# New orders at both ends of a fused attention and soft-MoE kernel, and queries loaded by one transfer per pair

## The chip, the cores and the metric

The kernel runs on one core of a Trainium2 chip. The metric is the device time in microseconds of one execution. A core has five engines with a queue of instructions each: TensorE (PE), VectorE (DVE), ScalarE (ACT), GpSimd (POOL) and SyncE (SP); SP does nothing here but issue transfers, which 16 DMA engines carry out. Engines wait for each other through semaphores.

## What is computed

Attention over 8 batches, 8 heads, 576 positions, 64 columns, where scores more than tau below their row's maximum are dropped, and then a soft mixture of experts over all 4608 positions (512 columns, 8 experts with 4 slots each, hidden size 1024):

```python
scores = scale * q @ k.T
thresh = scores.max(-1) - tau
scores = where(scores >= thresh, scores, -1e9)
attn = softmax(scores)
x = (attn @ v)                       # to (4608, 512)
logits = x @ phi                     # phi (512, 32)
d = softmax(logits, axis=0)          # over the 4608 positions
slot_input = d.T @ x                 # (32, 512)
for e in range(8):                   # 4 slots each
    slot_out[e] = relu(slot_input[e] @ w1[e]) @ w2[e]
c = softmax(logits, axis=1)
out = c @ slot_out                   # (4608, 512)
```

## The kernel before

The 64 heads are worked off as 32 pairs of heads, the two heads of a pair in the two halves of the 128 partitions, or with one half for each half of the keys. Pair p of batch b = p // 4 has nine groups of queries. Per group: PE multiplies q by k (L776; the ninth group L781) into one of four PSUM regions; DVE copies the scores out with the sign turned and takes the row's extreme (L788); ACT takes the exponential (L798); POOL makes the threshold (L801); DVE masks and sums (L804). Then PE transposes the weights (recorded at L692), ACT copies them to pTa, pTb and pTl (L697), and PE multiplies them by v (L894), 256 and 320 queries at a time. The result is transposed back, scaled and kept as x and xT. After the fourth pair of a batch the dispatch follows: logits (L976), running maximum (L982, L985), exponentials dT and f (L989, L987), weighing of x into acc (L1024, L1029, L1037). When the last batch is done, the slot inputs (L948) are made and the tail starts, in an order written by hand: hidden layer (L1200), second layer (L1234), combination (L1276), stores.

Loads: q, k and vv have two buffers each. The load of a pair's q waits for the last q·k product of the pair two before it, k's likewise, and vv's for the last product with v. All loads after the first pair's stand in SP's queue, one after the other: what is behind a waiting load waits too. DMA semaphores go round eight, so a load also waits for the landing of the eighth before it. k is loaded in two halves (L740, 64 rows of 2 x 288) and then scaled by POOL (L756). q has the same 64 rows in both halves of the partitions, since the two halves of the array work on different keys with the same queries. 26 of 64 weight tiles of 512 KB are preloaded during the attention (w, L672); 20 more (host) go into attention buffers that have become free, and 18 follow into w buffers after their first use.

The order: every instruction up to the tail is put down with `G.add(engine, duration, nominal time, function, reads, writes)` in the class Order. `plan()` sorts each engine's instructions by a number, from TABLE where there is one, places them one by one and gives out the buffers. So TABLE's numbers are a fixed order for each engine's queue, SP's included, and nothing is moved at run time. The planner counts 4500 ns from an SP issue to its data for every load, whatever its shape (`LAT`). TABLE is keyed by scopes: "first" and "last" for the first and last pair, "pair0" to "pair3" for the middle ones (with a, y, z for the first and the last two batches), "batch", "end", "load..", "new..", and "soft" for the softmax over the slots. FILL (14 double) and WARM (17 single) are 128x128 transposes of the identity without use for the result, placed on PE at the start and near the end.

The queries of a pair, in before:

```python
for g in range(2 if p else 0):
    G.add("SP", 1250 if p < 3 else 800, t0 - 18 + hs[0], lambda g=g, a=hs[0], z=hs[-1] + 1: nc.sync.dma_start(
        qt.t[rows[g], a:z], qT[b, j, :, a:z]), w=[qt[h, g] for h in hs])
```

where `rows` is the two halves of the partitions, `qT[b, j]` is 64 x 2 x 576 and `qt` is a tile of 128 x 2 x 576.

Of the kernel before, what the change touches and what calls it, by code (L numbers as in the profile page):

```python
# [34 lines left out]
WARM = 17  # L35
# [3 lines left out]
for _n, _v in (  # L39
    ("first", [  # L40
# [7 lines left out]
    ]),  # L48
# [8 lines left out]
    ]),  # L57
# [8 lines left out]
    ]),  # L66
# [9 lines left out]
    ]),  # L76
# [476 lines left out]
def softmax_attention_soft_moe(  # L553
# [815 lines left out]
```

## Time and profile before

| | |
|---|---|
| time, median of 3 runs | 546.99 us (546.82 to 549.59) |
| profiled execution | 546.67 us |
| its span | 544.9 us (1.8 us lie around it) |
| PE, DVE, ACT, POOL busy | 524.9, 469.6, 456.9, 243.4 us |
| loaded and stored by DMA | 83.03 MB, 152 GB/s in the mean |
| first product q·k on PE | 5.68 us |
| hidden layer begins (L1200) | 482.28 us |

In a row of time the first number is the start in us from the begin of the span, the second the duration; then come engine, line, operation, what is written and what is read (`out<-in`), shape and count. In brackets stands how long the engine was idle before and what released it. SPq is the issue of a transfer on SP's queue; the transfer itself comes later. Matmuls are pipelined and their ends are modelled, so rows of PE overlap a little.

### The profile page before, as it was taken

To read this page: it belongs to the slowest core of one execution; us is meant where nothing else is said; L and a number is where in the kernel's file an instruction comes from. 1 tells how busy PE (TensorE), PEld (TensorE's weight loads), DVE (VectorE), ACT (ScalarE), POOL (GpSimd) and SP (SyncE) were. 2 spreads that over 40 slices of the span, in tenths; PEclk is the share of its full clock that TensorE was granted. 3 is DMA by queue.
4 is the path that set the end of the run, shared out by engine and by line. 5 is a ranking of instruction groups with operands and counts; after the bars stand their busy time and mean duration, and the time that the engine had idled before them with its cause. 6 is when DMAs were issued, how large, how long until landed. Compare 5 with 4: busy or idle time off the path is not lost.

```text
span 544.9 us, 18241 instructions
## 1 busy us (share of the span) xinstructions
PE 524.9 (96%) x6994; PEld 335.8 (62%) x6994; DVE 469.6 (86%) x1326; ACT 456.9 (84%) x786; POOL 243.4 (45%) x475
## 2 busy tenths in 40 slices
PE   8999999999999999999999999999999999999990
PEld 6666666666666666666666666666666656644470
DVE  6999998999999999999899989999999999522192
ACT  3999998999899989998999989999999888621180
POOL 3554555554545454545355545545454624121030
PEclk9999999999999999999999999999999999999996
DMA  7256555555535553333233333333333303999498
GB/s 182 69 165 172 168 167 169 165 164 165 174 91 168 166 161 119 96 85 91 71 91 92 90 92 92 91 91 91 91 91 92 89 5 141 348 410 410 188 371 321
DMA packets 31990, 83.03 MB, mean 152 GB/s; under 512 B 4640, under 2 KB 12832, under 8 KB 31904
## 3 DMA queue, kind: packets, MB, share of 16 engines
q1 hardware_dynamic: 31584, 81.43, 48.6%
q8 instruction: 55, 0.90, 0.7%
q10 hardware_dynamic: 320, 0.44, 0.3%
q14 instruction: 31, 0.25, 0.2%
HBM read 72.42 MB, written 9.44 MB: 150 GB/s over the span
## 4 chain that ended last, share of the span: by engine, by line
PE 86%; ACT 5%; DVE 5%; issue 2%; DMA 1%; SPq 0%; DVEq 0%; ACTq 0%
PE ps L894 29%; PE ps L776 24%; PE ps L692 17%; PE ps L781 3%; PE h L1200 3%; PE so L1234 2%; PE ps L918 2%; PE ps L976 2%; PE ps L1024 1%; DVE p L804 1%; ACT pTb L697 1%; DVE cT L1192 1%; DVE host L1280 1%; ACT pTa L697 1%; ACT p L798 1%
## 5 line engine op out<-in xcount | busy, mean ns | idle before, releaser
L788 DVE TENSOR_SCALAR_CACHE_REDUCE ss<-ps 128x576 f32<-128x576 f32 x288 | 208.3, 751 | 15.5 <-ACT pTl L697 4.8
L801 POOL TENSOR_SCALAR thr<-nmx,pabs 128x1 f32<-128x1 f32 x288 | 132.6, 462 | 185.0 <-DVE ss L788 164.8
L804 DVE SCALAR_TENSOR_TENSOR p<-ss,thr,p 128x576 f32<-128x576 f32 x256 | 201.3, 821 | 4.0 <-ACT p L798 3.8
L798 ACT ACTIVATE p<-ss,nmx 128x576 f32<-128x576 f32 x256 | 188.1, 780 | 15.1 <-DVE ss L788 15.0
L776 PE MATMUL ps<-k,q 64*128 64x288 f32 x1024 | 167.1, 427 | 1.4 <-DMA q<-in_qT 0.5
L692 PE MATMUL ps<-ident,p 64*128 64x64 f32 x2304 | 97.7, 223 | 1.3 <-ACT pTa L697 1.0
L692 PEld LDWEIGHTS ps<-ident,p 64*128 64x128 f32 x2304 | 88.0, 138 | 17.5 <-ACT pTa L697 3.1
L776 PEld LDWEIGHTS ps<-k,q 64*128 64x128 f32 x1024 | 83.3, 188 | 22.6 <-ACT pTl L876 5.8
L697 ACT COPY pTb<-ps 128x1024 f32<-128x1024 f32 (+1 forms) x96 | 84.0, 876 | 5.0 <-PE ps L692 3.1
L894 PE MATMUL ps<-pTb,vv 128*64 128x320 f32 x512 | 76.0, 439 | 0.4 <-DVE pTl L876 0.4
L697 ACT COPY pTa<-ps 128x1024 f32<-128x1024 f32 x64 | 64.9, 1017 | 0.4 <-PE ps L692 0.4
L894 PE MATMUL ps<-pTa,vv 128*64 128x256 f32 x512 | 62.3, 385 | 0.0
L894 PEld LDWEIGHTS ps<-pTb,vv 128*64 128x64 f32 x512 | 34.1, 136 | 36.4 <-issue 8.9
L894 PEld LDWEIGHTS ps<-pTa,vv 128*64 128x64 f32 x512 | 34.0, 136 | 26.2 <-DVE ss L788 8.5
L894 PE MATMUL ps<-pTl,vv 128*64 128x256 f32 (+1 forms) x256 | 41.9, 406 | 0.0
L913 POOL TENSOR_TENSOR x<-x,ri 128x512 f32<-128x512 f32 x31 | 32.3, 1042 | 4.7 <-ACT x L697 4.7
L697 ACT COPY xT<-ps 128x256 f32<-128x256 f32 (+1 forms) x62 | 24.7, 398 | 6.3 <-PE ps L894 5.3
L894 PEld LDWEIGHTS ps<-pTl,vv 128*64 128x64 f32 x256 | 18.5, 137 | 12.6
L804 DVE SCALAR_TENSOR_TENSOR pL<-ss,thr,pL 128x576 f32<-128x576 f32 x32 | 26.0, 813 | 0.0
L798 ACT ACTIVATE pL<-ss,nmx 128x576 f32<-128x576 f32 x32 | 24.8, 775 | 0.5 <-DVE ss L788 0.5
L1169 POOL TENSOR_TENSOR c<-lall,crow 128x512 f32<-128x512 f32 x9 | 9.3, 1046 | 35.5 <-PE ct L684 35.5
L756 POOL TENSOR_SCALAR k<-k,flag 128x576 f32<-128x576 f32 x31 | 25.1, 809 | 0.2
(137 smaller groups left out, 536.8 us busy)
## 6 DMA issues: line engine op xcount, KB each, us to landing
w<-in_w SPq DMA_DIRECT2D x44, 512.0 KB, 7.0
q<-in_qT SPq DMA_DIRECT2D x62, 288.0 KB, 4.6
vv<-in_vt SPq DMA_DIRECT2D x32, 320.0 KB, 4.9
host<-in_w SPq DMA_DIRECT2D x20, 512.0 KB, 7.4
k<-in_kT SPq DMA_DIRECT2D x62, 144.0 KB, 3.1
out<-w SPq DMA_DIRECT2D x8, 512.0 KB, 3.7
out<-host SPq DMA_DIRECT2D x8, 512.0 KB, 5.1
out<-host SPq DMA_DIRECT2D x4, 256.0 KB, 4.5
```

The lines of the kernel that those rows point to most:

```text
L692: nc.tensor.transpose(out=s[:, g, c:c + 64], in_=ins[g], identity=ident[rows[g], rows[g]], tile_position=(64 * g, 0))
L697: G.add("ACT", 51 + 0.833 * n, nom, lambda: nc.scalar.copy(*io()), r, w)
L756: sc = lambda e, kc=kc: lambda: e.tensor_scalar(out=kt.t[:, kc], in0=kt.t[:, kc], scalar1=flag8, **one)
L776: nc.tensor.matmul(s.t[:, g, 0:HS], qt.t[rows[g], h, c * 128:(c + 1) * 128], kt.t[rows[g], h * HS:(h + 1) * HS], start=True, stop=True, ti ...
L781: nc.tensor.matmul(s.t[rows[a], g, 0:HS], qt.t[rows[g], a, SM:S], kt.t[rows[g], a * HS:(a + 1) * HS], start=True, stop=True, tile_position ...
L788: dve(674, t + OFF['mx'], [s], [ss, nmx], lambda s=s, ss=ss, nmx=nmx: nc.vector.tensor_scalar(out=ss.t.rearrange("p (a k) -> p a k", a=2), ...
L798: G.add("ACT", 668, t + OFF['ex'], lambda sv=sv, nmx=nmx, view=view: nc.scalar.activation(view().rearrange("p (a k) -> p a k", a=2), sv(), ...
L801: pool(250, t + OFF['th'], lambda nmx=nmx, thr=thr: nc.gpsimd.tensor_scalar(out=thr.t, in0=nmx.t, scalar1=1.0, scalar2=pabs, op0=ALU.mult, ...
L804: fn=lambda sv=sv, thr=thr, view=view, i=i: nc.vector.scalar_tensor_tensor(out=view().rearrange("p (a k) -> p a k", a=2), in0=sv(), scalar ...
L894: nc.tensor.matmul(lone(w)[h * 64:(h + 1) * 64, 0:n], vv.t[:, v0:v0 + 64], p0, start=(kb == 0), stop=(kb == 4), tile_position=(0, h * 64), ...
L913: G.add("POOL", 1040, u + 6.8, own=f"new{j}" + group(b), r=[ri[0]], w=[x[j]], fn=lambda: nc.gpsimd.tensor_tensor(out=wide(), in0=wide(), i ...
L1200: nc.tensor.matmul(hp[n][g * 32:(g + 1) * 32, :], siT[:, kb, :], t[g][:, n * 512:(n + 1) * 512], start=(kb == 0), stop=(kb == 3), tile_pos ...
```

## The change

Three things change: TABLE's numbers for the first and the last pair, for the dispatch and the softmax, for the loads and for the middle pairs too; WARM; and the load of q.

```diff
-WARM = 17
+WARM = 13
...
     ("first", [
-        -29145.8, -29045.8, 5200, -28845.8, -28745.8, -28645.8, 7150, 3900, 6450, 7520, 8376, 8414, 16050.4, 9956,
+        -18044.4, -29045.8, 5200, -12489.2, -28745.8, -26707.8, 7150, -12484.5, 6450, 7520, -17331.8, 7943.7, 17078.1,
...
-            for g in range(2 if p else 0):
-                G.add("SP", 1250 if p < 3 else 800, t0 - 18 + hs[0], lambda g=g, a=hs[0], z=hs[-1] + 1: nc.sync.dma_start(
-                    qt.t[rows[g], a:z], qT[b, j, :, a:z]), w=[qt[h, g] for h in hs])
+            if p:
+                G.add("SP", 1250 if p < 3 else 800, t0 - 18, lambda: nc.sync.dma_start(
+                    qt.t.rearrange("p h s -> p (h s)"),
+                    qT[b, j].rearrange("d h s -> d (h s)").unsqueeze(0).to_broadcast([2, D, 2 * S])),
+                    w=[qt[h, g] for h in hs for g in range(2)])
+                G.skip(1)
```

Before, each of the two transfers reads 64 rows of 1152 floats from memory and writes 64 partitions. After, one transfer reads the pattern 2 (step 0) x 64 x 1152 and writes 128 partitions. `G.skip(1)` keeps the numbering for TABLE. The new lines move the rest of the file by one or two lines, so L776 is L777 in after, L754 is L752, L740 is L738, L761 is L762, L672 is L670, L692 is L690 and L976 is L977.

SP's queue at the start, in before, from the loads of pair 1 on (k_262 and q_266 are the buffers of pair 1, k_302 and q_306 those of pairs 0 and 2; x2 is two issues in a row):

```order
L740 DMA k_262<-in_kT 64x2x288 x2
L754 DMA q_266<-in_qT 64x1152
L761 DMA vv_190<-in_vt 128x640
L754 DMA q_266<-in_qT 64x1152
L1073 DMA phi_sb<-in_phi 128x4x32
L740 DMA k_302<-in_kT 64x2x288 x2
L754 DMA q_306<-in_qT 64x1152 x2
```

and in after (q_258 and k_254 are pair 1's):

```order
L752 DMA q_258<-in_qT 128x1x1152
L738 DMA k_254<-in_kT 64x2x288 x2
L752 DMA q_306<-in_qT 128x1x1152
L738 DMA k_302<-in_kT 64x2x288 x2
L762 DMA vv_190<-in_vt 128x640
L762 DMA vv_282<-in_vt 128x640
```

q goes ahead of k, pair 2's q ahead of pair 1's vv, and phi moves back by some ten rows.

SP's queue near the end, in before (q_266 is of pairs 29 and 31, q_306 and k_302 of pair 30, vv_286 of pair 28, vv_190 of pair 29):

```order
L754 DMA q_266<-in_qT 64x1152 x2
L761 DMA vv_286<-in_vt 128x640
L740 DMA k_302<-in_kT 64x2x288 x2
L754 DMA q_306<-in_qT 64x1152 x2
L761 DMA vv_190<-in_vt 128x640
L754 DMA q_266<-in_qT 64x1152
```

and in after (q_258 is of pairs 29 and 31, q_306 and k_302 of pair 30, vv_282 of pair 28):

```order
L752 DMA q_258<-in_qT 128x1x1152
L752 DMA q_306<-in_qT 128x1x1152
L762 DMA vv_282<-in_vt 128x640
L762 DMA vv_190<-in_vt 128x640
L738 DMA k_302<-in_kT 64x2x288 x2
L752 DMA q_258<-in_qT 128x1x1152
```

Pair 28's vv, which stood ahead of pair 30's k and q, now stands behind pair 30's q, and pair 30's k behind both vv.

DVE's queue after the last pair's masks, in before (ss is the spread reciprocal, xT and x the last pair's result, M the running maximum, msel the table for the last scale):

```order
L899 TENSOR_TENSOR xT_178<-ps_327,ss_186 128x256
L899 TENSOR_TENSOR xT_178<-ps_326,ss_186 128x320
L982 TENSOR_REDUCE M_162<-ps_328 128x1
L701 COPY x_142<-ps_325 128x2x4x64
L985 TENSOR_REDUCE M_154<-M_162 128x1
L1008 TENSOR_REDUCE msel<-ps_325 128x32
```

and in after:

```order
L1060 TENSOR_REDUCE crow<-lall 128x31
L824 COPY ss_186<-ps_328 64x64
L1063 TENSOR_SCALAR crow<-crow 128x31
L1070 RECIPROCAL crow<-crow 128x31
L824 COPY ss_186<-ps_328 64x64
L900 TENSOR_TENSOR xT_178<-ps_326,ss_186 128x256
L900 TENSOR_TENSOR xT_178<-ps_327,ss_186 128x320
L983 TENSOR_REDUCE M_158<-ps_325 128x1
L986 TENSOR_REDUCE M_154<-M_158 128x1
L699 COPY x_142<-ps_328 128x2x4x64
```

The second maximum goes ahead of the copy of x, and the sum of the softmax over the slots of the first seven batches (crow, 128x31) with its reciprocal comes here; before, it stood some 35 rows earlier. On ACT the last batch's d is now copied ahead of f. In both orders eight w tiles are loaded per batch, from pair 5 on in before and a little later in after.

More of the change, by code (lines that the diff above doesn't have):

```diff
@@ L40 @@
     ("first", [
[7 rows of a table removed]
[7 rows of a table added]
     ]),
     ("pair0", [
[7 rows of a table removed]
[7 rows of a table added]
     ]),
     ("pair1", [
[7 rows of a table removed]
[7 rows of a table added]
     ]),
     ("pair2", [
[8 rows of a table removed]
[7 rows of a table added]
     ]),
     ("pair3", [
[7 rows of a table removed]
[7 rows of a table added]
     ]),
     ("last", [
[7 rows of a table removed]
[7 rows of a table added]
     ]),
     ("new0", [
-        42772.8, 45402.2, 46047.2,
+        44643, 45017, 45018.3,
     ]),
     ("new1", [
-        41998, 44523.2, 45168.2,
+        42453.1, 44432.3, 45229.6,
     ]),
     ("new2", [
-        39785.1, 43601.1, 44246.1,
+        40108.5, 42725.5, 44307.4,
     ]),
     ("new3", [
-        39398.4, 43285.9, 43930.9,
+        39770.4, 43137.2, 46021.3,
     ]),
     ("end", [
[3 rows of a table removed]
[3 rows of a table added]
     ]),
     ("batch", [
-        32102.4, 32769.7, 30644.4, 32436.4, 32832.4, 33247.2, 33658.1, 33447.2, 35553.8, 35963.4, 35284.8, 35805.8,
-        36407.6, 37744.8, 38581.8, 36599.8, 38004.8,
+        32177.1, 33414.8, 30661.9, 30802.5, 34331.7, 36709.2, 33602.8, 33671, 34935.5, 35685.3, 34984.3, 36285.3,
+        38203.2, 37705.9, 38579.7, 37294.6, 38533.2,
     ]),
     ("soft", [
-        -20145.8, -17727.1, -15712.2, -13865.5, -12089.8, -11250.8,
+        -20202.1, -18866.8, -72.6, 3460.8, 10192.9, 11209.2,
     ]),
@@ L121 @@
     ]),
-    ("load20", [
-        -9471.2,
+    ("batchy", [
+        34714.2, 32911, 35125.6, 29604.8, 30540.9, 34650.8, 34640.9, 34650.9, 37923.5, 36031.1, 37587.7, 35502.5,
+        30636.8, 39086.2, 32599.8, 40425.9, 36369.6,
+    ]),
+    ("load8", [
+        -10710.3,
     ]),
     ("pair1a", [
[7 rows of a table removed]
[7 rows of a table added]
+    ]),
+    ("load9", [
+        -10120.3,
+    ]),
+    ("load24", [
+        -10708.4,
+    ]),
+    ("load0", [
+        -5147.2,
+    ]),
+    ("load19", [
+        -8002.1,
+    ]),
+    ("load4", [
+        -9473,
+    ]),
+    ("new2a", [
+        40084.7, 43396.6, 44304.6,
+    ]),
+    ("load2", [
+        -9857.3,
+    ]),
+    ("loadf8", [
+        12312,
+    ]),
+    ("loadf6", [
+        11876,
+    ]),
+    ("loadf3", [
+        11077,
+    ]),
[8 rows of a table added]
+    ]),
+    ("load17", [
+        -10119.3,
+    ]),
+    ("load12", [
+        -9472.1,
     ]),
@@ L136 @@
     ]),
-    ("load10", [
-        -8593.1,
+    ("load22", [
+        -10393.3,
+    ]),
+    ("loadf9", [
+        12530,
+    ]),
+    ("load7", [
+        -9805.2,
+    ]),
[8 rows of a table added]
+    ]),
+    ("load21", [
+        -8881.2,
+    ]),
+    ("loadw", [
+        16378.1, 16632.1, 16741.1, 16850.1, 16959.1, 17275.1, 17798.1, 18321.1, 20216.1, 20520.1, 20629.1, 20738.1,
+        21747.1, 21856.1, 21965.1, 22074.1, 22183.1, 22292.1, 22401.1, 22510.1, 22619.1, 22728.1,
+    ]),
[8 rows of a table added]
+    ]),
+    ("load13", [
+        -8882.1,
+    ]),
[8 rows of a table added]
+    ]),
[8 rows of a table added]
+    ]),
+    ("new3a", [
+        39470, 43257.1, 46695.5,
+    ]),
+    ("load16", [
+        -10709.3,
+    ]),
+    ("new2z", [
+        32119.2, 33767.6, 36800.3,
+    ]),
[8 rows of a table added]
+    ]),
+    ("new0z", [
+        49900.3, 48097.6, 45843.9,
+    ]),
+    ("load1", [
+        -4557.2,
+    ]),
+    ("new3y", [
+        38415.4, 43124.2, 41602.8,
+    ]),
+    ("loadf13", [
+        14833,
+    ]),
+    ("new1y", [
+        41759, 44499.9, 45232.4,
+    ]),
+    ("loadf2", [
+        9593,
+    ]),
+    ("loadh", [
+        0, 10, 20, 30, 40, 50, 60, 70, 80, 90, 100, 110, 120, 130, 140, 150, 160, 170, 180, 190,
+    ]),
+    ("load14", [
+        -10394.2,
+    ]),
+    ("loadf7", [
+        12094,
     ]),
@@ L143 @@
     ("pair0y", [
[7 rows of a table removed]
-    ]),
-    ("new1a", [
-        41995.2, 44520.4, 45165.4,
-    ]),
[8 rows of a table removed]
-    ]),
-    ("loadh", [
-        0, 10, 20, 30, 40, 50, 60, 70, 80, 90, 100, 110, 120, 130, 140, 150, 160, 170, 180, 190,
-    ]),
-    ("load1", [
-        -4557.2,
-    ]),
-    ("load14", [
-        -10394.2,
-    ]),
[8 rows of a table removed]
-    ]),
-    ("new3y", [
-        39401.2, 43288.8, 43933.8,
[7 rows of a table added]
+    ]),
+    ("load3", [
+        -9267.3,
     ]),
@@ L197 @@
     ]),
[8 rows of a table removed]
+    ("load25", [
+        -10118.4,
+    ]),
+    ("loadf10", [
+        13393,
+    ]),
+    ("loadf11", [
+        13756,
+    ]),
+    ("loadf0", [
+        0,
+    ]),
+    ("load18", [
+        -8592.1,
+    ]),
+    ("load10", [
+        -8593.1,
     ]),
@@ L209 @@
     ]),
-    ("new2z", [
-        32224.6, 33793.6, 36536.6,
-    ]),
[8 rows of a table removed]
-    ]),
-    ("load19", [
-        -8002.1,
-    ]),
-    ("loadf10", [
-        13393,
-    ]),
-    ("load17", [
-        -10119.3,
-    ]),
-    ("new3a", [
-        39395.5, 43283.1, 43928.1,
-    ]),
[8 rows of a table removed]
-    ]),
-    ("load3", [
-        -9267.3,
-    ]),
-    ("loadf6", [
-        11876,
-    ]),
-    ("load8", [
-        -10710.3,
-    ]),
-    ("load21", [
-        -8881.2,
-    ]),
-    ("loadf8", [
-        12312,
-    ]),
-    ("loadf13", [
-        14833,
-    ]),
-    ("new1y", [
-        42000.9, 44526, 45171,
-    ]),
-    ("loadf7", [
-        12094,
-    ]),
-    ("new0y", [
-        42775.7, 45405.1, 46050.1,
-    ]),
-    ("load2", [
-        -9857.3,
-    ]),
-    ("load12", [
-        -9472.1,
-    ]),
-    ("new1z", [
-        35804.7, 38846, 39491,
-    ]),
-    ("load22", [
-        -10393.3,
-    ]),
-    ("loadf1", [
-        8109,
-    ]),
-    ("loadf11", [
-        13756,
-    ]),
-    ("load9", [
-        -10120.3,
-    ]),
-    ("load13", [
-        -8882.1,
-    ]),
-    ("new0z", [
-        42571.7, 46041.9, 46686.9,
-    ]),
[8 rows of a table removed]
-    ]),
-    ("new2a", [
-        39782.3, 43598.2, 44243.2,
-    ]),
-    ("new2y", [
-        39788, 43603.9, 44248.9,
[8 rows of a table added]
+    ]),
+    ("load20", [
+        -9471.2,
     ]),
@@ L314 @@
     ]),
-    ("loadf0", [
-        0,
-    ]),
-    ("load16", [
-        -10709.3,
-    ]),
[9 rows of a table removed]
-    ]),
-    ("load18", [
-        -8592.1,
+    ("new1a", [
+        42096.7, 43675.1, 44195.8,
+    ]),
+    ("new0a", [
+        29817.1, 33155.9, 36170.4,
+    ]),
+    ("batcha", [
+        31502.8, 33983.6, 30044.8, 31282.4, 33831.4, 33795.5, 35033.9, 36691.3, 36147.9, 37567.3, 38292.2, 37778.2,
+        38715.1, 37060.4, 38682.2,
     ]),
@@ L368 @@
     ]),
-    ("load25", [
-        -10118.4,
-    ]),
-    ("new0a", [
-        31415.3, 32922.4, 34027.2,
-    ]),
-    ("loadf2", [
-        9593,
-    ]),
-    ("loadf3", [
-        11077,
+    ("new1z", [
+        35961.5, 36979, 39554.7,
+    ]),
+    ("new2y", [
+        41879.8, 43610.7, 44142.7,
+    ]),
+    ("new0y", [
+        42708.1, 45379, 46111.4,
+    ]),
[8 rows of a table added]
+    ]),
+    ("loadf1", [
+        8109,
     ]),
```

28 lines of the change are left out of this document (removed), and 246 rows, old and new, of the table TABLE.

## The prediction

> **What bounds the kernel now.** I read the page first, then the stages by windows, then TensorE and the SP queue in order of time, and last the DMA answers by line. The page's head, its slices and the shares of its chain of waits:
>
> ```profile
> span 544.9 us, 18241 instructions
> PE 524.9 (96%) x6994; PEld 335.8 (62%) x6994; DVE 469.6 (86%) x1326; ACT 456.9 (84%) x786; POOL 243.4 (45%) x475
> ...
> DMA  7256555555535553333233333333333303999498
> GB/s 182 69 165 172 168 167 169 165 164 165 174 91 168 166 161 119 96 85 91 71 91 92 90 92 92 91 91 91 91 91 92 89 5 141 348 410 410 188 371 321
> ...
> PE 86%; ACT 5%; DVE 5%; issue 2%; DMA 1%; SPq 0%; DVEq 0%; ACTq 0%
> ```
>
> TensorE (PE) is the bound: 96% busy and 86% of the chain. The DMA engines have room in the attention, less so in the last 80 us. The windows say the same by stage:
>
> ```profile
> 0.00:20.00 20.00, 17.29 (x153) 12.30 (x155) 15.09 (x48) 11.28 (x16) 7.92 (x19) 1.00 0.64 154
> 20.00:40.00 20.00, 19.32 (x248) 12.34 (x246) 19.46 (x58) 18.14 (x32) 11.67 (x21) 1.00 0.45 126
> 200.00:220.00 20.00, 20.00 (x330) 13.02 (x328) 18.02 (x53) 18.84 (x34) 9.69 (x18) 1.00 0.53 155
> 440.00:460.00 20.00, 19.24 (x268) 12.20 (x262) 19.23 (x52) 18.39 (x31) 8.02 (x17) 1.00 0.27 97
> 480.00:500.00 20.00, 20.00 (x179) 8.95 (x181) 3.75 (x10) 3.97 (x8) 5.33 (x21) 1.00 1.03 409
> ```
>
> The first number behind the window's length is PE's busy time; the last three are the granted clock, the DMA share and GB/s. In the middle PE has no idle time at all, so new orders can win only at the two ends, and any new wait of PE for a load is paid in full. All 16 DMA engines together move 409 GB/s at a share of 1.03, so one engine moves 409/16 = 25.6 GB/s. That is the price that the rest hangs on.
>
> How the queries come now, in the middle (SP's queue), and TensorE beside it:
>
> ```profile
> 214.87 1.58 SPq L740 DMA_DIRECT2D k<-in_kT  x2
> 216.50 1.23 SPq L754 DMA_DIRECT2D q<-in_qT  x2
> 217.84 0.53 SPq L761 DMA_DIRECT2D vv<-in_vt  x1
> ```
> ```profile
> 202.61 1.53 PE L976 MATMUL ps<-xT,phi_sb 128*32 128x128 f32 x64
> ...
> 213.62 1.19 PE L776 MATMUL ps<-k,q 64*128 64x288 f32 x8
> ...
> 232.05 0.70 PE L776 MATMUL ps<-k,q 64*128 64x288 f32 x4
> ...
> 260.20 1.53 PE L976 MATMUL ps<-xT,phi_sb 128*32 128x128 f32 x64
> ```
>
> L976 comes once per batch of four pairs, so a batch takes 260.20 - 202.61 = 57.6 us. There are two q buffers: the load for a pair waits for the last q·k product (L776) of the pair two before it, here in the group at 213.62, and the next product from that buffer is the group at 232.05. So a load issued at 216.5 has about 15 us. It needs far less:
>
> ```profile
> q<-in_qT SPq DMA_DIRECT2D x62, 288.0 KB, 4.6
> vv<-in_vt SPq DMA_DIRECT2D x32, 320.0 KB, 4.9
> ...
> k<-in_kT SPq DMA_DIRECT2D x62, 144.0 KB, 3.1
> ```
>
> **The queries, part by part.** The edit takes away 31 DMA issues on SP (0.6 us each, from 1.23 for two; SP is not late, so worth nothing). In their place stands one transfer of 576 KB whose destination is 128 rows, but whose source is written as 2 copies (step 0) of 64 rows. Every load of the kernel before has an outermost count of 64 or 128 on both sides; this one has 2 on its source side. No row of before shows how such a transfer is divided among the 16 engines, so I bound it. With all 16, 589,824 bytes / 409 GB/s = 1.4 us, less than two halves cost now. Divided along its outermost count, into two parts of 64 rows on two engines: 294,912 bytes / 25.6 GB/s = 11.5 us on each. I take the second end: a transfer has to be cut along a dimension that both its patterns have, and the outermost one is what every other load here could be cut along.
>
> [...]
>
> What 11.5 us does is a matter of rows. All loads are on the one SP queue, and an engine works off its pieces in turn, so k, vv and w, which are spread over 16 engines, land only after their pieces on the two loaded engines. Per batch these two carry 4 q x 11.5 = 46.0; 8 k x 9,216 bytes = 8 x 0.36 = 2.9; 4 vv x 0.80 = 3.2; together 52.1 us. While the w tiles are preloaded (26, eight per batch in both orders, so 3.25 batches) 8 x 1.28 = 10.2 more: 62.3 us, above the 57.6 that a batch takes. Besides, the engines idle from the moment a buffer comes free to the first byte:
>
> ```profile
> DMA to landing us min/median/max: 2.7/3.1/5.1
> ```
>
> This is L740's answer: a k half lands 2.7 us after its issue at the earliest, of which 0.4 is its own transfer: 2.3 us of start. Four such starts per batch are 9.2 us, or nothing where the other buffer's load is still flowing. The batch with w thus takes between 62.3 and 71.5 us; I take 67, the middle, as if half of the loads found the other still under way: 9.4 more than now, x 3.25 = **+30.5**. A batch without w takes between 57.6 and 52.1 + 9.2 = 61.3; here engines mostly idle when a buffer comes free, so I take 61.3: +3.7 x 3.75 batches = **+14**.
>
> At the start, the rows of before are:
>
> ```profile
> 4.24 0.58 SPq L761 DMA_DIRECT2D vv<-in_vt  x1
> 4.87 1.31 SPq L740 DMA_DIRECT2D k<-in_kT  x2
> ```
> ```profile
> 15.32 1.19 PE L776 MATMUL ps<-k,q 64*128 64x288 f32 x8
> ...
> 17.15 0.83 PE L692 MATMUL ps<-ident,p 64*128 64x64 f32 x20 [0.65 <-ACT pTa L697]
> ...
> 28.20 1.19 PE L776 MATMUL ps<-k,q 64*128 64x288 f32 x8
> 29.22 0.41 PE L692 MATMUL ps<-ident,xT 64*128 64x64 f32 x8
> 29.97 0.72 PE L692 MATMUL ps<-ident,p 64*128 64x64 f32 x16 [0.34 <-ACT pTa L697]
> ```
> ```profile
> L756 POOL TENSOR_SCALAR k<-k,flag 128x576 f32<-128x576 f32 x31 | 25.1, 809 | 0.2
> ```
>
> In the new order q of pair 1 stands at 4.87, with k of pair 1 behind it. Its bytes start behind vv's, by 9 us, and land at about 20.8; k's pieces 0.7 later; the scaling of k on GpSimd (L756) takes 0.8: pair 1's first product at 22.4, where TensorE would reach it at about 17 (now inside the group at 15.32; the new order has some more transposes of pair 0 ahead): +5.4. Pair 2's q waits in the same rings to 33.0, then k and L756: 34.6 against the 28.20 of the row, +6.4. Pair 3's q waits for pair 1's last product, then 2.3 + 11.5 + 1.5 more. The first batch loses 9 to 16; I take **+12**.
>
> At the end the new order also puts vv of pair 28 right behind q of pair 30, which waits for pair 28's last product:
>
> ```profile
> 414.01 0.70 PE L776 MATMUL ps<-k,q 64*128 64x288 f32 x4
> ...
> 422.02 1.95 PE L894 MATMUL ps<-pTa,vv 128*64 128x256 f32 x16
> ```
>
> In before this first use of vv comes 8.0 us after that product; 0.6 + 2.3 + 11.5 + 0.8 = 15.2 are needed, of which some delay of TensorE in between is off: **+6.5**.
>
> **The orders.** With four fewer warm-up transposes (WARM 17 to 13; 0.12 us each) and transposes of other pairs ahead of the wait at 17.15, I count 0.8 of the 1.0 us of the two stalls at 17.15 and 29.97 as gone. At the end the second long sum of the softmax over the slots leaves a place where DVE is crowded, for one after the last masks:
>
> ```profile
> 445.67 1.18 DVE L1059 TENSOR_REDUCE crow<-lall 128x31 f32<-128x992 f32 x1
> ```
> ```profile
> 471.08 2.93 PE ps L894 x20
> ...
> 475.54 0.69 DVE x L701
> 476.33 0.42 ACT dT L989
> ...
> 477.38 0.29 ACT f L987
> 477.70 0.38 ACT d L697
> ```
>
> and in the last chain the small reduce that dT waits for is put ahead of the copy of x (up to 0.69), and d ahead of f (0.29): about 1.2 us earlier to the hidden layer. There the weights stream at the full 409 GB/s, so perhaps a tenth of it to half of it reaches the end. Together -1 (0 to -3).
>
> **The sum.** The profiled execution took 546.67 us, 0.3 below the median of 546.99: 546.7 + 30.5 + 14 + 12 + 6.5 - 1 = 608.7, rounded **608 us**. Its bounds: 62.3 per laden batch and nothing in the others gives 546.7 + 15 + 9 - 3 = 568; 71.5 per laden batch, 16 at the start and another stall of 6.5 at the end gives 546.7 + 45 + 14 + 16 + 13 = 635.
>
> **The rivals.**
>
> *Sixteen engines after all* (0.15), which is not slower. The transfer is then 1.4 us and lands like a q of now (4.6 us, under 15 us of cover); only the orders count. Start -0.8; end 0 to -1.2, capped by the weights at 409 GB/s: 545.6, with at most a few stalls more that put it at 548, or up to 4 us of the end's stalls gone: 542.5. For it: nothing in before ever ran on fewer engines. Against it: the count of 2.
>
> *Two engines, but hidden* (0.05). With 13.8 us from issue to landing and about 15 us of cover, q alone would pass; the price is the start's 9 to 12 and the end's 6.5: about 562. It decides whether k and vv wait behind q. Against it: all are on one queue, and the 62.3 us per laden batch exceed 57.6.
>
> *Two engines, and slower ones* (0.05). The window 200:220 moves 155 GB/s at a share of 0.53: 155 / (16 x 0.53) = 18.3 GB/s per busy engine. At this rate q takes 16.1 us, four are 64.4, and with the rest and the starts a batch takes 80 to 90: 546.7 + 7 x 27 = 736. Against it: that window's halves of 64 rows come from 16 engines at once into half of the partitions; two engines alone don't meet that.
>
> **How the numbers follow.** The forecast has 0.75. About 0.5% is what a measurement of this kernel can tell from no change. Slower by more than that: 0.75 + 0.05 + 0.05, and 0.01 of the sixteen-engine case with new stalls: 0.86. The rest of that case: 0.11 within 0.5%, 0.03 faster. The range takes in the forecast's bounds, widened above by 25 us for what a queue held up by two engines may cost beyond the sums, and below to the hidden case: 560 to 660. It leaves out the sixteen-engine and the slow-engine cases (0.20).
>
> **What would show it.** Right: the DMA answer for q (L752) with a median over 13 us to landing; the DMA share in the middle near 2 engines' work and far below now's GB/s; PE waiting for DMA q, POOL k or vv in the chain of waits, in the first place at about 17 us; batches (L977) 61 to 70 us apart, the longer ones while w is loaded. Wrong: q landing within 5 us, and batches still 57.6 us apart; then the time lies near 546, and only the gaps at both ends have moved.

## The result, and the profile after

Six runs of the changed kernel have a median of 665.94 us, six of the kernel before 547.65 us, taken in turn: a ratio of 1.215 (95% interval 1.211 to 1.218). The prediction of 608 us had the direction, the two engines, and half of the size; 666 lies above its range.

The page's head of the changed kernel, its slices, packets and the shares of its chain of waits:

```profile
span 664.0 us, 18109 instructions
PE 558.8 (84%) x6990; PEld 364.8 (55%) x6990; DVE 476.8 (72%) x1326; ACT 461.7 (70%) x786; POOL 229.6 (35%) x475
...
PEclk9797997889889978989989989999996979899996
DMA  3222223425251441525221222231221202389968
...
DMA packets 31060, 83.02 MB, mean 125 GB/s; under 512 B 3710, under 2 KB 11902, under 8 KB 30974
...
DMA 41%; PE 40%; DVE 5%; issue 5%; ACT 4%; SPq 2%; POOL 2%; DVEq 0%; POOLq 0%; ACTq 0%
DMA q<-in_qT 26%; PE ps L895 13%; PE ps L777 11%; DMA k<-in_kT 10%; PE ps L690 7%; DMA host<-in_w 3%; DMA vv<-in_vt 2%; PE so L1235 2%; PE ps L782 1%; SPq L738 1%; ACT p L799 1%; DVE p L805 1%; DVE ss L789 1%; PE h L1201 1%; POOL thr L802 1%
```

The chain, 86% PE before, now goes through the loads of q and k for more than a third. The 119 us more in the span are 85 of idle time on PE (664.0 - 558.8 = 105, against 20) and 34 more of busy time for almost the same instructions, because the granted clock falls: its mean over the span is 0.923, against 0.990 before, and it is 0.50 for 104.4 us, against 12.4. The DMA row is lower than before in most slices; but it is a mean over 16 engines and can't show two of them that are busy.

What PE waits for, in total, times and longest:

```profile
PE ps L777 <- DMA q<-in_qT: 28.3, 10, 5.8
PE ps L777 <- issue: 24.1, 7, 6.8
PE ps L777 <- POOL k L757: 10.3, 2, 5.9
PE ps L895 <- DMA vv<-in_vt: 8.6, 1, 8.6
PE ps L919 <- DVE ss L789: 6.0, 1, 6.0
```

The waits put down to "issue" are for q too: the trace lacks the landing of those transfers, but it keeps every DMA packet with its start, length and size, and only q's after pair 0 have 4608 bytes. The last packet of a q ends 0.55 us before the product in six of these seven waits. The next rows are the long pieces of the chain of waits for a stretch of the middle (start, length, what): a q is waited for over 20 us from its issue, the pair's products follow, and the issue of the next q is released by the last of them.

```profile
202.01 22.77 DMA q<-in_qT
224.79 0.14 issue
224.92 0.76 PE ps L777 x4
...
235.43 0.58 SPq L670
236.01 0.05 issue
236.06 20.58 DMA q<-in_qT
```

The logits come once per batch. Here are two of the eight rows in time, and from all of them what each batch takes now and took before:

```profile
110.07 1.53 PE L977 MATMUL ps<-xT,phi_sb 128*32 128x128 f32 x64
...
264.19 1.53 PE L977 MATMUL ps<-xT,phi_sb 128*32 128x128 f32 x64
```

| from the begin of the span, or per batch | before | after | more |
|---|---|---|---|
| first logits at | 87.2 | 110.07 | 22.9 |
| three batches with w tiles | 57.7, 57.7, 57.6 | 78.8, 75.3, 75.6 | 56.7 |
| two batches without | 57.6, 57.6 | 65.1, 66.0 | 15.9 |
| second last batch | 57.6 | 78.65 | 21.0 |
| last batch, then to the hidden layer | 36.1, 13.2 | 38.2, 12.1 | 1.0 |

That makes 117.6 (599.88 against 482.28 at the hidden layer) of the 119.1 us between the two spans; the rest lies in the tail.

### The profile page after: what moved, and what is told of

Same layout as the page of the kernel before. It is cut to its first block, busy times and chain, and to the rows that moved or that the text cites. A ratio compares the mean times of both kernels' runs of the same rounds, so it can differ in the third digit from the quotient of the medians.

```text
span 664.0 us, 18109 instructions
## 1 busy us (share of the span) xinstructions
PE 558.8 (84%) x6990; PEld 364.8 (55%) x6990; DVE 476.8 (72%) x1326; ACT 461.7 (70%) x786; POOL 229.6 (35%) x475
## 2 busy tenths in 40 slices
DMA packets 31060, 83.02 MB, mean 125 GB/s; under 512 B 3710, under 2 KB 11902, under 8 KB 30974
## 4 chain that ended last, share of the span: by engine, by line
DMA 41%; PE 40%; DVE 5%; issue 5%; ACT 4%; SPq 2%; POOL 2%; DVEq 0%; POOLq 0%; ACTq 0%
DMA q<-in_qT 26%; PE ps L895 13%; PE ps L777 11%; DMA k<-in_kT 10%; PE ps L690 7%; DMA host<-in_w 3%; DMA vv<-in_vt 2%; PE so L1235 2%; PE ps L782 1%; SPq L738 1%; ACT p L799 1%; DVE p L805 1%; DVE ss L789 1%; PE h L1201 1%; POOL thr L802 1%
## 5 line engine op out<-in xcount | busy, mean ns | idle before, releaser
L777 PE MATMUL ps<-k,q 64*128 64x288 f32 x1024 | 184.7, 466 | 68.4 <-DMA q<-in_qT 28.3
L805 DVE SCALAR_TENSOR_TENSOR p<-ss,thr,p 128x576 f32<-128x576 f32 x256 | 205.9, 835 | 22.6 <-POOL thr L802 19.4
L802 POOL TENSOR_SCALAR thr<-nmx,pabs 128x1 f32<-128x1 f32 x288 | 118.2, 415 | 228.7 <-DVE ss L789 198.6
L777 PEld LDWEIGHTS ps<-k,q 64*128 64x128 f32 x1024 | 96.0, 207 | 95.3 <-issue 54.1
L690 PEld LDWEIGHTS ps<-ident,p 64*128 64x128 f32 x2304 | 95.8, 145 | 21.3 <-issue 5.9
L690 PE MATMUL ps<-ident,p 64*128 64x64 f32 x2304 | 103.1, 230 | 2.8 <-DVE p L805 2.5
L895 PE MATMUL ps<-pTb,vv 128*64 128x320 f32 x512 | 82.9, 470 | 0.0
L895 PE MATMUL ps<-pTa,vv 128*64 128x256 f32 x512 | 64.4, 395 | 8.8 <-DMA vv<-in_vt 8.6
L895 PEld LDWEIGHTS ps<-pTb,vv 128*64 128x64 f32 x512 | 36.1, 145 | 37.0 <-issue 9.7
L895 PEld LDWEIGHTS ps<-pTa,vv 128*64 128x64 f32 x512 | 35.0, 140 | 35.4 <-issue 10.2
L914 POOL TENSOR_TENSOR x<-x,ri 128x512 f32<-128x512 f32 x31 | 34.6, 1115 | 21.4 <-ACT x L695 21.2
L836 POOL TENSOR_SCALAR pL<-pL,ri 128x576 f32<-128x576 f32 x31 | 24.5, 789 | 27.4 <-DVE ri L832 26.2
L695 ACT COPY pTl<-ps 128x256 f32<-128x256 f32 x64 | 23.8, 372 | 12.8 <-PE ps L690 12.4
```

What stands on the lines that cost most here:

```text
L690: nc.tensor.transpose(out=s[:, g, c:c + 64], in_=ins[g], identity=ident[rows[g], rows[g]], tile_position=(64 * g, 0))
L695: G.add("ACT", 51 + 0.833 * n, nom, lambda: nc.scalar.copy(*io()), r, w)
L777: nc.tensor.matmul(s.t[:, g, 0:HS], qt.t[rows[g], h, c * 128:(c + 1) * 128], kt.t[rows[g], h * HS:(h + 1) * HS], start=True, stop=True, ti ...
L802: pool(250, t + OFF['th'], lambda nmx=nmx, thr=thr: nc.gpsimd.tensor_scalar(out=thr.t, in0=nmx.t, scalar1=1.0, scalar2=pabs, op0=ALU.mult, ...
L805: fn=lambda sv=sv, thr=thr, view=view, i=i: nc.vector.scalar_tensor_tensor(out=view().rearrange("p (a k) -> p a k", a=2), in0=sv(), scalar ...
L836: pool(725, t + OFF['sc'], lambda k=k, view=view_: nc.gpsimd.tensor_scalar(out=view(), in0=view(), scalar1=ri.t[:, k:k + 1], **one), [ri[c ...
```

## The experiments

### Which part, and how many engines

Every pair's queries again in two transfers, with the new orders left in:

```diff
-G.add("SP", 1250 if p < 3 else 800, t0 - 18, lambda: nc.sync.dma_start(
-    qt.t.rearrange("p h s -> p (h s)"),
-    qT[b, j].rearrange("d h s -> d (h s)").unsqueeze(0).to_broadcast([2, D, 2 * S])),
+G.add("SP", 1250 if p < 3 else 800, t0 - 18, lambda: [nc.sync.dma_start(
+    qt.t[rows[g]], qT[b, j]) for g in range(2)],
```

> The kernel after with q of a pair in two transfers of 64 rows again, issued together at the place of the one; all orders are those of after. Theory (the one transfer is worked off by 2 of the 16 DMA engines, and that is all of the loss): 545.6 us, between 542.5 and 548, batches 57.6 us apart, granted clock 0.99, as many packets under 512 B as before (4640). Rival (the new orders cost it, above all q ahead of k and vv behind q on SP's queue): over 600 us.

Measured: 547.19 us, ratio 0.9982 (0.9966 to 0.9999). The orders gain 1.2 us up to the hidden layer (481.0 against 482.3 us), of which nothing shows in the span (545.0 against 544.9); that the tail, which streams weights at 409 GB/s, takes it back fits, but no run tests it. No version of the study is clearly faster than this one, and its own gain is at the edge of what can be measured.

The other half of the change: the orders of before, with q by one transfer (the change's own lines).

> The kernel before with its own orders and WARM 17, and only the load of q as in after (one transfer, source 2 x 64 rows). On SP k stands ahead of q in nearly all pairs here. Theory: the loss is there without the new orders, 620 to 665 us, batches with w 66 to 77 us apart; a little less than after, since the products wait for q but seldom for k behind it. Rival (the new orders cost it): below 560 us.

Measured: 644.42 us, ratio 1.174 (1.171 to 1.177), batches 75.6, 75.1, 67.5, 64.5, 65.2, 65.1. So the transfer alone makes nearly all of the loss. The new orders, harmless with two halves, cost another 21.5 us with the one transfer, 13.6 of them in the second last batch (78.65 against 65.1).

One transfer of the same bytes to the same 128 partitions, but from a q that lies twice in memory, so that both sides have 128 rows outermost:

```diff
-    qt.t.rearrange("p h s -> p (h s)"),
-    qT[b, j].rearrange("d h s -> d (h s)").unsqueeze(0).to_broadcast([2, D, 2 * S])),
+    qt.t, qT[b, j]),
...
-    qT=pair(q), ...
+    qT=np.concatenate([pair(q)] * 2, axis=2), ...
```

> The kernel after, still with one transfer of 576 KB per pair, but q lies twice in memory, so that the source has 128 rows of its own as outermost dimension. Theory (2 engines because the outermost count is 2): 16 engines again, q lands within 5 us, the time of e1 within 1 us. Rival (one transfer of 576 KB to all 128 partitions is slow by its size): over 620 us, q landing after 13 us or more.

Measured: 548.26 us, ratio 0.9996 (0.9981 to 1.001), all batches 57.7. One transfer instead of two is neither a gain nor a loss.

Next the count alone, without any step of 0: q lies in memory (laid out so among the inputs) as groups of rows, with a gap between them so that they can't be merged into one dimension; two groups of 64, four of 32, eight of 16.

```diff
-    qT[b, j].rearrange("d h s -> d (h s)").unsqueeze(0).to_broadcast([2, D, 2 * S])),
+    qt.t.rearrange("p h s -> p (h s)"), qT[b, j, :, 0:64]),        # then 0:32, 0:16
...
+qq = np.concatenate([pair(q)] * 2, axis=2).reshape(B, HP, 2, 64, 2 * S)   # then 4, 32 and 8, 16
+qq = np.concatenate([qq, qq[:, :, :, 0:1]], axis=3)
```

> The kernel after with one transfer per pair whose source is 2 groups of 64 rows that lie apart in memory (q twice, a spare row behind each group), so without a step of 0. Theory (the outermost count sets the engines): as after, 660 to 672 us, 3710 packets under 512 B. Rival (the repeated reading of the same rows, step 0, does it): 545 to 549 us.

> The same with 4 groups of 32 rows. Theory: 4 engines, 5.8 us for q on each, 3772 packets under 512 B; a load lands 8 us after its issue, or up to 16 where w, vv and the other q are ahead of it, against some 12 to 18 us until its first use: 547 to 556 us. If engines are not set by the count: as e5.

> The same with 8 groups of 16 rows. Theory: 8 engines, 2.9 us for q on each, 3896 packets under 512 B, everything hidden: 546 to 549 us, no wait of TensorE for q in the middle.

Measured: 665.1, 578.89 and 553.09 us. The copy as such is thus not the cause: two groups that really lie apart cost the same as two that are one. Against the expectation four engines still cost 5.6%, and eight 0.8%: 2.3 us up to the first logits and 3.2 in the second last batch, with 57.7 in between. The packets tell the count directly. Two rows of the pages, of before and of the version with q twice in memory:

```profile
DMA packets 31990, 83.03 MB, mean 152 GB/s; under 512 B 4640, under 2 KB 12832, under 8 KB 31904
```
```profile
DMA packets 31494, 83.02 MB, mean 152 GB/s; under 512 B 4144, under 2 KB 12336, under 8 KB 31408
```

62 transfers have become 31, and 496 = 31 x 16 small packets are gone: one per transfer and engine. On that reading the 62 halves have 992 of the 4640, and each of the other versions leaves 3648 plus 31 times its count of engines:

| q's outermost count | packets under 512 B | engines, (packets - 3648) / 31 | time, us | ratio |
|---|---|---|---|---|
| 128 (twice in memory) | 4144 | 16 | 548.26 | 0.9996 |
| 8 | 3896 | 8 | 553.09 | 1.008 |
| 4 | 3772 | 4 | 578.89 | 1.056 |
| 2, apart | 3710 | 2 | 665.10 | 1.213 |
| 2, step 0 (the change) | 3710 | 2 | 665.94 | 1.215 |

### What sets a batch of 75 us

The prediction priced a batch by the work on the two loaded engines. With the one transfer for odd pairs only, that work falls far below the batch:

```diff
-    ....to_broadcast([2, D, 2 * S])),
+    ....to_broadcast([2, D, 2 * S])) if p % 2 else [
+        nc.sync.dma_start(qt.t[rows[g]], qT[b, j]) for g in range(2)],
```

> The kernel after with the one transfer for odd pairs only and two transfers for even pairs: 15 more issues on SP. The two loaded engines carry 2 x 11.5 + 2.9 + 3.2 + 10.2 = 39 us per batch of 57.6. If full engines make the loss: 547 to 556 us. If it is that q lands 14 us or more after its issue and k and vv wait behind it: 570 to 610 us, about half of the loss.

Measured: 635.62 us, ratio 1.158 (1.154 to 1.161). Half of the transfers cost three quarters of the loss, and both expectations fail. The batches with w take 76.0, 73.8 and 73.1 us, and the next, in which a single w tile loads, still 70.9, so that eight w tiles are not needed for it. The rows of the second of these, from logits to logits, on PE and then on SP:

```profile
185.22 1.53 PE L978 MATMUL ps<-xT,phi_sb 128*32 128x128 f32 x64
...
206.31 3.25 PE L778 MATMUL ps<-k,q 64*128 64x288 f32 x12 [5.01 <-DMA q<-in_qT]
...
223.08 1.68 PE L778 MATMUL ps<-k,q 64*128 64x288 f32 x12
...
241.34 1.33 PE L778 MATMUL ps<-k,q 64*128 64x288 f32 x4 [5.91 <-issue]
...
243.28 3.23 PE L778 MATMUL ps<-k,q 64*128 64x288 f32 x12
...
259.01 1.53 PE L978 MATMUL ps<-xT,phi_sb 128*32 128x128 f32 x64
```
```profile
186.93 0.56 SPq L752 DMA_DIRECT2D q<-in_qT  x1
...
218.41 1.34 SPq L738 DMA_DIRECT2D k<-in_kT  x2
219.81 0.58 SPq L670 DMA_DIRECT2D w<-in_w  x1
220.44 1.41 SPq L763 DMA_DIRECT2D vv<-in_vt  x2
221.90 0.55 SPq L752 DMA_DIRECT2D q<-in_qT  x1
...
260.72 0.55 SPq L752 DMA_DIRECT2D q<-in_qT  x1
```

All three of these q share one buffer, and the two turns from issue to issue are 34.97 and 38.82 us, together 73.79. That this is the batch, 259.01 - 185.22 = 73.79, proves nothing yet, since any buffer is loaded twice per batch. One turn is: q is issued, the pair's first product comes some 19 us later (186.93 to 206.31, 221.90 to 241.34), its products run, the last one frees the buffer, and SP issues what stands ahead in its queue (here k, w and vv, 3.5 us from 218.41 to 221.90) before the next q. What makes it the limit is that this chain has little slack: PE stands still ahead of the pair's first product in both turns, 5.01 and 5.91 us (the second is put to "issue"; q's last packet ends 1.5 us before its end), and SP waits for the buffer. Nor are the two loaded engines full: for 21.2 us of this batch fewer than two packets are under way on all 16.

The changed kernel has two such turns side by side, one per buffer. The buffer of the rows at 202.01 and 236.06 above is issued next at

```profile
278.04 0.54 SPq L752 DMA_DIRECT2D q<-in_qT  x1
```

two turns of 34.05 and 41.98 us: 76.0, where its batches take 75.3 and 75.6. Here, though, fewer than two packets are under way for only 7.2 us of the batch of 75.3, so its two engines may have been busy for 68. In the changed kernel itself the work on the engines and the turn of the buffers lie close together, and no run tells them apart; the run with odd pairs shows that the turn suffices.

The packets also divide the landing. Of the twelve q of the three batches with w, the first packet starts 3.1 to 9.6 us after the issue, and the last ends 16.7 to 21.8 us after it. The packets take 11.7 to 13.5 us of each engine, 12.55 in the mean, which is 23.5 GB/s. So most of what exceeds the forecast's 13.8 us is waiting for the first packet, the longer waits being those of a q with the other buffer's q ahead of it.

Does the low clock lengthen the turn? The rows above say that it can: twelve products of one shape take 1.68 us at 223.08 and 3.23 at 243.28, behind the wait (granted clock 1.00 from 222 to 226 us, 0.50 from 243 to 246), and such products are part of the turn. Two runs were to measure it: 24 transposes of the identity (without use for the result) ahead of one group's product in each pair, to keep PE busy while it waits; then 450 of them only for the 15 pairs where it had idled over 2 us.

```diff
 def qk(i=i, c=c, h=h, s=s):
+    for n in range(24 if p and i == 0 else 0):
+        nc.tensor.transpose(out=s.t[:, n % 2, 384:512], in_=ident, identity=ident)
```

> The kernel after with 24 transposes of the identity (0.11 us each, 2.7 in all) on TensorE ahead of the first q.k product of each pair from pair 1 on; their result is overwritten. They need no load, so they run while TensorE waits for q, and where it doesn't wait they cost 2.7 us. Theory (besides the waits, the halved clock after a wait costs some 34 us of TensorE's time): the time at half clock falls from 104 us to under 40, and the time to 635 to 660 us in spite of the work added. Rival (the loads alone set the time, the clock is only a sign of it): 666 us or more.

> The kernel after with such transposes only ahead of the first product of the 15 pairs where TensorE stood idle for 2 us and more in the trace of after, as many as filled nine tenths of that wait at full clock (18 to 52 each, 466 in all, some 52 us), so that they add next to nothing of their own. Theory (the halved clock after a wait costs up to 34 us): time at half clock from 104 us to under 50, the time 635 to 655 us. Rival (the loop of the loads sets the time, whatever the clock): 660 to 672 us.

Measured: 681.95 us (ratio 1.240) and 678.37 us (1.239), slower than the changed kernel by 16 and 12 us. The first gives its rival's time (666 us or more), the second neither. The mean granted clock rose from 0.923 to 0.965 and 0.944, yet the batches with w stayed at 77.0, 75.1, 75.2 and 75.5, 75.6, 75.4 us (78.8, 75.3, 75.6 without the transposes). But the edit doesn't do what was meant. TABLE puts another group's product first in most pairs, so that the transposes stand behind the wait. Two rows of the second run, at pair 1:

```profile
22.20 1.33 PE L779 MATMUL ps<-k,q 64*128 64x288 f32 x4 [5.97 <-POOL k L757]
...
28.86 5.24 PE L776 MATMUL ps<-ident 128*128 128x128 f32 x46
```

In that run the transposes fill the wait for pairs 7, 11 and 15 alone, and seven waits of 2.5 us or more stay. So the transposes add work to the turn while the clock takes some away, and the clock's share isn't settled. What the first run does show is that PE had room: its busy time in the second batch with w rose from 62.6 to 71.2 us at the same length.

Then q from another queue, so that it doesn't stand behind SP's other loads:

```diff
-G.add("SP", 1250 if p < 3 else 800, t0 - 18, lambda: nc.sync.dma_start(
+G.add("ACT", 620, t0 - 8 - 13 * (p == 1), lambda: nc.scalar.dma_start(
```

> The kernel after with the same one transfer per pair on 2 engines, but issued from ScalarE's queue at the place where its buffer comes free, and not from SP's: k, vv and w no longer stand behind q in one queue. The orders of the other engines are those of after. Theory (k, vv and w waiting behind q, and q behind w, make a good part of the loss): batches with w 60 to 68 us instead of 75 to 79, in all 590 to 625 us. Rival (the 11.5 us of q itself on two engines make it): 645 us and more.

Measured: 702.82 us, ratio 1.284 (1.280 to 1.288), batches with w 92.5, 88.7, 88.7: the theory misses, and the rival's time holds. PE waits for q over 60.5 us in 14 waits, and now for vv over 30.1 us in 4. The issue itself stands in order among ScalarE's own work here, with semaphore waits of only 0.02 to 0.04 us at its line, so this doesn't tell how much of the 19 us is queueing. It does tell that ScalarE's queue, used like this, is no way out. vv, still on SP, is late all the same: 30.1 us of waiting, against 8.6 in the changed kernel.

### The transfer or its neighbours

The one transfer for pairs 11 and 25 only, in a kernel that otherwise has two halves:

```diff
-    ....to_broadcast([2, D, 2 * S])),
+    ....to_broadcast([2, D, 2 * S])) if p in (11, 25) else [
+        nc.sync.dma_start(qt.t[rows[g]], qT[b, j]) for g in range(2)],
```

> The kernel after with the one transfer for pairs 11 (while w is loaded) and 25 (after that) alone, two transfers for all others. Theory: pair 25's load lands some 14 us after its issue and is hidden; pair 11's, with w, vv and k on the same engines, lands after 16 to 20 us and makes TensorE wait 0 to 3 us: 547 to 550 us. If any load on two engines is a loss of 3 us as the mean over 31 pairs would have it: 553 us or more.

Measured: 555.72 us, ratio 1.0154 (1.013 to 1.0178): two transfers of 31 cost 8 us, 6.9 in the batch of pair 11, where w tiles load, and 1.7 in that of pair 25, where none do. The time is above the theory's, and the two costs are too different for the rival's even 3 us per load. PE before pair 11, and three of the clock's windows (the number before the last two is the granted clock):

```profile
165.56 3.16 PE L778 MATMUL ps<-k,q 64*128 64x288 f32 x12 [5.28 <-issue]
```
```profile
156.00:160.00 4.00, 4.00 (x58) 2.44 (x56) 4.00 (x13) 3.87 (x7) 2.80 (x5) 1.00 0.60 164
...
164.00:168.00 4.00, 2.44 (x10) 2.02 (x12) 0.80 (x3) 0.19 (x1) 0.05 (x1) 0.64 0.15 55
168.00:172.00 4.00, 4.00 (x44) 2.37 (x40) 3.81 (x11) 3.27 (x5) 2.77 (x5) 0.94 0.06 20
```

A wait of 5.28 us makes the batch longer by 6.9 (64.6 against 57.7): behind the wait PE runs at a lower clock for a while, 0.64 and 0.94 in two windows of 4 us, which is a clock of 0.50 for some 3.4 us ((0.36 + 0.06) x 4 / 0.5, an estimate). The changed kernel's trace has this too: its granted clock is always 1.00 or 0.50, and all 15 stretches at 0.50 ahead of the tail's last 10 us begin within a wait of PE or up to 1.2 us after it, the first, from 18.9 to 25.7 us, within the wait of 5.94 us before pair 1.

On SP, k, vv and two w stood ahead of this q (issued at 142.95 to 145.45, q at 145.93). So pair 11 alone has the one transfer next, and first of all:

```diff
+if p == 11:
+    G.add("SP", 800, t0 - 42.628, bc, w=qw, own="q11")     # bc: the one transfer
```

> The one transfer for pair 11 alone (pair 25 too has its two again), and on SP it stands ahead of k, vv and w of that stretch, first of what is issued when pair 9's last product has freed the buffer. Theory: in the run with pairs 11 and 25, pair 11's q was issued at 145.93, 3 us after the first k that the same product freed (142.95), with vv and two w tiles ahead of it in the same rings, and landed some 19.6 us after its issue, 5.3 us too late. Put first it is issued near 143 and its two engines are nearly empty: 143 + 2.3 + 11.5 = 157, ahead of the 160.3 at which TensorE wants it, and k, behind it in the rings, about 1 to 2 us later with its scaling. TensorE's wait before pair 11 falls from 5.3 us to 0 to 1.5, that batch from 64.6 to 57.7 to 59.5 us, the time to 547 to 550. Rival: 11.5 us on two engines are too long for the cover of 14 us wherever the transfer stands, since k, vv and w then wait behind it: the batch stays at 62 to 65 us, the time at 552 to 555.

Measured: 554.45 us, ratio 1.0122 (1.010 to 1.0143), that batch 64.4 us: the rival's numbers, and not quite its story. Now k, behind q in the same engines, is late (first the trace's answer on the line of k, for its two halves, in us from issue to landing; then PE; then windows):

```profile
DMA to landing us min/median/max: 16.7/16.8/17.0
```
```profile
165.06 0.69 PE L925 MATMUL ps<-ident,x 64*128 64x64 f32 x8 [4.26 <-POOL x L920]
```
```profile
148.00:152.00 4.00, 4.00 (x52) 2.49 (x54) 3.96 (x13) 3.95 (x12) 1.67 (x3) 1.00 0.95 249
152.00:156.00 4.00, 4.00 (x76) 2.44 (x68) 3.53 (x9) 3.63 (x7) 0.53 (x2) 1.00 0.92 277
164.00:168.00 4.00, 2.94 (x34) 2.66 (x36) 3.89 (x9) 1.87 (x3) 3.07 (x5) 0.50 0.79 188
```

Where k stands ahead of q, two runs on, the same two halves land 2.9 us after their issue. GpSimd waits 6.9 us to scale k, in order, so the pair before gets its threshold and its x late (L920), and PE stalls on a transpose for that pair. And q was slow itself: while the w tiles load, a busy engine moves 249 / (16 x 0.95) = 16 to 277 / (16 x 0.92) = 19 GB/s, not the 25.6 that the prediction took. Its own packets agree here: 15.4 us of each of the two engines, 19.1 GB/s.

So k was put ahead of q again and the five w tiles around it behind the next pair's loads:

```diff
-    G.add("SP", 800, t0 - 42.628, bc, w=qw, own="q11")
+    G.add("SP", 800, t0 - 42.6247, bc, w=qw, own="q11")
...
-G.add("SP", 590, (i // 2 + 3) * N9, lambda i=i: load_unit(wslots[i]), ...)
+G.add("SP", 590, 75.3562 + (i - 8) * .0001 if 8 <= i <= 12 else (i // 2 + 3) * N9, lambda i=i: load_unit(wslots[i]), ...)
```

> As before the one transfer for pair 11 alone, now with its k ahead of it on SP, nothing else in flight, and the five w tiles that stood around it moved behind the loads of the next pair; vv alone follows it. Theory: by itself the transfer needs 2.3 us to start and 11.5 us on its two engines; issued at about 144.5 to 145.3 it lands at 158.3 to 159.5, before TensorE wants it at 160.3, and neither k nor w waits behind it. TensorE's wait before pair 11 goes to 0 to 1.5 us, that batch from 64.4 to 57.7 to 59.5 us, the time to 547 to 550. Rival: it needs longer than its cover even when it is alone (two engines carry less than 25.6 GB/s each into 128 partitions, or vv behind it is what is missed): a wait of 3 to 6 us stays before pair 11 or at vv's first use, the batch at 61 to 65 us, the time at 551 to 555.

Measured: 554.71 us, ratio 1.0116 (1.0086 to 1.0146). The time and, nearly, the batch (65.1) are the rival's, the place is neither's. PE no longer waits before pair 11, and does before pair 13 (the rows of their first products; the bracket is the wait):

```profile
160.35 1.73 PE L783 MATMUL ps<-k,q 64*128 64x288 f32 x12
...
191.26 1.30 PE L783 MATMUL ps<-k,q 64*128 64x288 f32 x2 [3.57 <-DMA q<-in_qT]
```

The five w tiles, 2.6 MB in one pile, now delay the two halves of pair 13: the chain has 14.30 us from issue to landing, where the median of before is 4.6, and from 180 to 184 us the DMA engines move 409 GB/s at a share of 1.02. That is a fault of the experiment, so two more runs spread the five over later pairs without w, one with pair 11's queries in one transfer and one with two halves at the same place:

```diff
-G.add("SP", 590, 75.3562 + (i - 8) * .0001 if 8 <= i <= 12 else ...
+G.add("SP", 590, 75.3562 + (i - 2) * 9 if 8 <= i <= 12 else ...
...
-    G.add("SP", 800, t0 - 42.6247, bc, w=qw, own="q11")
+    G.add("SP", 800, t0 - 42.6247, lambda: [              # in the second run
+        nc.sync.dma_start(qt.t[rows[g]], qT[b, j]) for g in range(2)], w=qw, own="q11")
```

> As the run before, but the five w tiles taken from around pair 11 go to five later places, one or two per pair in the stretch that has no w, so that they don't pile up before pair 13 (there its q came 14.3 us after its issue, and TensorE waited 3.57 us). Theory: no wait before pair 11 as in the run before, none before pair 13, all batches 57.7 to 58.5 us, 547 to 549 us: a transfer on two engines costs nothing where its 16 us of cover hold it and nothing shares its engines. Rival: another wait appears behind the transfer or where the w tiles now go, a batch at 60 to 65 us, 550 to 555.

> The same places as the run with the w tiles in the later stretch, with pair 11's queries in two transfers like all the others. Theory: batches of 57.7, 547 to 548.5 us, and no measurable difference from that run. Rival: that run is slower than this one by 3 us or more, and the transfer itself costs it.

Measured: 547.38 us (ratio 0.9996, 0.9983 to 1.0009) and 548.18 us (1.0004, 0.9989 to 1.0018): no difference, all batches 57.7 to 58.0. SP and PE of the run with the one transfer, and then the time from issue to landing of the vv right behind it:

```profile
144.35 1.33 SPq L738 DMA_DIRECT2D k<-in_kT  x2
145.74 0.63 SPq L752 DMA_DIRECT2D q<-in_qT  x1
146.42 0.41 SPq L768 DMA_DIRECT2D vv<-in_vt  x1
```
```profile
161.53 1.67 PE L783 MATMUL ps<-k,q 64*128 64x288 f32 x12
```
```profile
DMA to landing us min/median/max: 14.5/14.5/14.5
```

The last packet of that q ends 13.4 us after its issue, and the product from it comes at 15.8 us, without a wait; vv behind it is held up to 14.5 us, and is not needed earlier. The same transfer at the same pair costs 6.9 us of a batch among its neighbours and nothing alone. Two things differ, the w tiles that were moved away and q's place ahead of vv; no run separates them.

## Why the prediction was right and wrong

**Two engines: right.** The cut along the outermost count of 2 is shown by the packets, and by the counts 2, 4, 8 and 128, which give the order of times. The destination had 128 rows in all of these, so it was the source's count that set the engines, with the step of 0 and without it. In the changed kernel's trace two of q's packets are under way at once for 344 of the 395 us in which any is. The prediction had no row that showed this and chose two engines by argument. The rival *sixteen engines* gave 545.6 for the orders alone; the measured ratio of 0.9982 makes 545.7 of the profiled 546.67 us.

**A batch with w at 67 us: this is the step that failed.** The prediction added up the work on the two loaded engines, 52.1 + 10.2 = 62.3, with at most four starts of 2.3, and took that as what sets the batch. The run with odd pairs only refutes the principle: with half of the q transfers that sum falls by some 20 us to about 42, 51 with the starts, and the batch took 73.8 where it should have kept its 57.6. What rules there is a loop with latency, one buffer's turn: landing, products, issue behind others, landing. Its products and issues stood in the trace of before, and the sum had them at nothing. The landing was forecast at 2.3 + 11.5 = 13.8 us, and a transfer alone on its engines does take 13.4; in the batches with w it takes 16.7 to 21.8, since the first packet starts 3.1 to 9.6 us after the issue and the packets take 12.55 us in the mean. The term was +30.5 for 3.25 batches; the three measured ones alone give 56.7. The rival *two slower engines* had a lower rate (18.3 GB/s) for all of the time, and its 736 us are far off: q's packets moved at 23.5. In the changed kernel the two engines may be busy for 68 of 75.3 us, 6 more than the sum had, so there the sum may have been too small in its own terms too.

**Batches without w: nearer.** 61.3 was forecast, 65.1 and 66.0 measured. Which of the two, the turn or the engines' work, sets these batches was not tested. (The sum's 608.7 should have been rounded to 609.)

**The start: right in its first step, short in the rest.** Pair 1's first product was forecast for 22.4 us, behind GpSimd's scaling of k:

```profile
22.57 1.33 PE L777 MATMUL ps<-k,q 64*128 64x288 f32 x4 [5.94 <-POOL k L757]
```

But +12 counted the first three pairs, and the first logits come 22.9 us late: pairs 5 and 6 wait too (1.6 and 2.8 us), and the clock falls (0.86 in the window from 20 to 40 us). How much the clock takes of this was not tested.

**The end: the named wait was right, its neighbours were missing.** vv of pair 28 behind q of pair 30 was put at 6.5 us and cost 8.6. The chain of that stretch has two more such places, k behind q:

```profile
488.05 14.30 DMA k<-in_kT
...
521.13 15.67 DMA vv<-in_vt
...
549.21 14.61 DMA k<-in_kT
```

With the first two, and PE's clock at 0.87, the second last batch grew by 21.0 us; the third lies in the last batch. With before's orders and the same transfer it grew by 7.5 (65.1), so two thirds of it come with the new orders, which put loads right behind q there.

**The orders at -1: right, as far as it can be measured.** -1.2 us by the hidden layer, none in the span.

**The clock: not in the prediction at all.** PE's busy time grew by 34 us. For a single stall in a saturated stretch it is a real term (5.28 us of waiting cost 6.9, 4.26 cost 6.7); in the batches that a buffer's turn sets, products at half of the clock lengthen the turn (3.23 us for 1.68), by how much in all stays open.

**"Two engines, but hidden": right only under conditions that the kernel doesn't have.** A transfer that lands in 13.4 us does go under 15.8 us of cover when its engines are otherwise nearly empty. With k, vv and w around it either it or what stands behind it is late. For all pairs the 562 us came to 666.

What stays open: the clock's share of a turn, and whether the changed kernel's own 75 us come from the turn or from two engines that are nearly full.

## What to carry to other kernels

Before two transfers are joined into one, look at the outermost count of the source's pattern: a count of 2 (copies or groups), 4 or 8 (groups) there left the one transfer of 128 rows on that many DMA engines here (ratios of 1.21, 1.056 and 1.008), and one transfer with 128 rows outermost cost no more than two halves (0.9996). When a load in a double-buffered loop becomes slow, price the buffer's turn (issue behind others, landing behind others, use, release) and not only the work of the engines: with half of the slow loads here the turn held the batch at 74 us, while the work on the engines summed to 42. And judge a slow transfer by its neighbours: what it delays behind it on the same engines cost as much here (6.7 us) as its own lateness (6.9).

## What the runs showed of the hardware that was not expected

- The small packets count engines: one under 512 B per transfer and engine (31 x 16, 31 x 8, 31 x 4, 31 x 2), so the page tells how many engines a transfer used.
- Transposes without use raised PE's mean granted clock from 0.923 to 0.965 in a kernel that became 16 us slower: a higher clock is no sign of a shorter time.
- Two engines moved q at 23.5 GB/s each in the changed kernel's batches with w and at 19.1 beside four w tiles in the run with pair 11's q first, against 25.6 at the full 409 GB/s of the tail.
- A transfer on two engines hardly shows in the DMA row of the page, which is a mean over 16: fewer than two packets were under way for only 7.2 us of a batch of 75.3 in which the mean share was 0.38.
